# First-batch value sums by block: values as the stationary operand, masks as the streaming one

## The chip, the cores and the metric

The kernel runs on one core of a Trainium2 chip. The time is the device time of one execution in microseconds (us). The engines are named as in the profile: PE is TensorE's matmul, PEld its weight load, DVE is VectorE, ACT is ScalarE, POOL is GpSimd, SP is SyncE, which here issues the DMAs. They run side by side; each takes its own instructions strictly in the order in which they were written, and waits where an operand is not there yet.

## The reference

Attention over 4 batches x 8 heads x 768 positions x 64 dimensions, each query seeing the keys within 16 positions and one summary for each block of 32 keys, followed by a feed-forward network on 3072 tokens. `moe(...)` is x @ w_in, then h * tanh(softplus(h)), then @ w_out.

```
k_sum = k.reshape(B, H, nb, block, D).max(axis=3)       # 24 blocks of 32
v_sum = v.reshape(B, H, nb, block, D).mean(axis=3)
scores = concat([where(|i-j| < 16, q k^T / 8, -1e9), q k_sum^T / 8 + log(32)])
a = softmax(scores)
out = moe(concat([v, v_sum]) weighted by a)
```

The change bears on `v_sum` of the first batch alone.

## The kernel before

Work is cut into units: a chunk `c` of 256 positions and a pair of heads `hp` (4 pairs, so 128 value columns). The first two chunks (group 0, 512 tokens) are prepared by functions of their own before the feed-forward steps can start. From some 46 us on, PE works through feed-forward steps (`ph`: `ff_in`, L445; `po`: `ff_out`, L473) with the attention of the later groups between them. The weights come as 64-bit words that DVE and ACT turn into a high and a low part; the low part is the last step (`G`, `lower_weight`, L176). The steps for one piece of weights are `f` (`scale_weight`, ACT, L151), `B` and `C` (DVE, L155 and L159), `cl` (`clamp_weight`, DVE, L163, which needs `f`), `E` (DVE, L168), `hi` (`upper_weight`, ACT, L173, which needs `E`), `G`.

The order is written out by hand as a list of words, `order`; each word is one call, and each engine gets its instructions in that order. The words that matter here:

- `vm0` to `vm3`: `first_value_sums` (L262). For head pair 0 to 3 it sums the values by block with matmuls on PE: 8 windows of 64 positions (96 rows with their margins) and 2 pieces of 128 positions.
- `vc0` to `vc3`: `first_value_summary` (L272). ACT copies the 24 sums x 128 columns out of PSUM into the last 24 rows of a tile `vm` whose other 96 rows POOL has set to zero at the start (`zeroed`, L204).
- `X0` to `X3`: `att_values` (L402 to L418). It needs that tile as the stationary operand of its L411 matmuls, and the transposed weights `pt`.
- `T`: `att_transpose` (L390), 4 transposes on PE out of POOL's normalised rows (`nm`, L384); `pc`: the copy of its result on ACT (L394); `a` and `b` before the pair's number are the two chunks.
- `S`: scores (L336, L338), `ttr`: their maxima on DVE (L353), `exp`: exponentials on ACT (L364), `rs`: divisors on DVE (L379, L380), `xh`, `xl`: high and low part of X (ACT L427, DVE L428).

In the list the stretch reads `vm0 lv2 hi0 rsa2 ttr9 G0 km3 vm1 vc0 Ta1 nm8 B1 X0 T8 rsb1 S3 nma2 expb2 exp9 lvw8 vc1 lv3 C1 f1 nmb1 cl1 ...`.

Of the kernel before, what the change touches and what calls it, by code (L numbers as in the profile page):

```python
# [58 lines left out]
def fused_kernel(ctx: ExitStack, tc: tile.TileContext, q0, qk, kt, v0, vw, vs, w_in, w_out, out):  # L59
    nc = tc.nc  # L60
    PS = bass.MemoryType.PSUM

# [119 lines left out]

    blocks = first_att.tile([P, NW + NR, NB], F32, tag="blocks", name="blocks", bufs=1)
    nc.gpsimd.memset(blocks, 1.0 / BLK)
    for part, step, at0 in ((blocks[:, :NW], QT, -WIN), (blocks[:, NW:], P, TG)):
# [1 line left out]
        nc.gpsimd.affine_select(
            out=part, in_=part, pattern=[[step, n], [-BLK, NB]], base=at0, channel_multiplier=1,  # L190
            compare_op=ALU.is_ge, fill=0.0)
# [3 lines left out]
    part = blocks[:, :NW]
    nc.gpsimd.affine_select(
        out=part, in_=part, pattern=[[0, NW], [0, NB]], base=-WIN, channel_multiplier=1,
        compare_op=ALU.is_ge, fill=0.0)
    nc.gpsimd.affine_select(
        out=part, in_=part, pattern=[[0, NW], [0, NB]], base=WIN + QT - 1, channel_multiplier=-1,  # L200
        compare_op=ALU.is_ge, fill=0.0)


    zeroed = []  # L204
    for hp in range(HP):
        zeroed.append(att.tile([KA, P], F32, tag="vm", name=f"vm0_{hp}", bufs=HP))
        nc.gpsimd.memset(zeroed[hp][0:KW], 0.0)
# [356 lines left out]
    order = """  # L564
        lk0 lk1 km1 km0 lqk8 lq0 S0 lq1 ttra0 S1 lk2 ttrb0 expa0 ttra1 lqk9 kc9 kc8 expb0 lw0 km2 rsa0 ttrb1 rsb0 S8
        nma0 Ta0 lq2 nmb0 ttr8 lv0 expa1 expb1 S2 f0 B0 rsa1 C0 pca0 lv1 cl0 Tb0 lk3 lw1 ttra2 ttrb2 E0 exp8 rs8 lq3
        expa2 nma1 pcb0 vm0 lv2 hi0 rsa2 ttr9 G0 km3 vm1 vc0 Ta1 nm8 B1 X0 T8 rsb1 S3 nma2 expb2 exp9 lvw8 vc1 lv3 C1 f1
        nmb1 cl1 pca1 Tb1 rsb2 pc8 ttra3 E1 rs9 xh0 pcb1 vm2 ttrb3 lw2 X1 expa3 X8 hi1 xl0 G1 vc2 lqk11 nmb2 Ta2 nm9 Tb2
        xh1 T9 xl1 expb3 lqk10 vm3 rsa3 nma3 pca2 pcb2 X2 xh8 ls12 lvw9 kc11 lw3 f2 Ta3 rsb3 B2 nmb3 C2 vc3 xh2 Tb3 kc10
        pca3 xl8 cl2 E2 pcb3 hi2 S10 xl2 km12 ttr10 X3 pc9 xh3 X9 exp10 G2 xl3 ls13 ttr11 B3 lw4 ph0 f3 ph1 C3 exp11 ph2  # L570
        cl3 xh9 mi0 E3 km13 xl9 hi3 ah0 rs10 ph3 mi1 lw5 ah1 B4 G3 al0 f4 C4 cl4 E4 mi2 al1 hi4 nm10 B5 G4 po0 mi3 f5 C5
        lvw11 po1 T10 ph4 cl5 E5 lqk13 lqk12 lt12 hi5 vq12 ph5 ah3 ah2 al3 rs11 pc10 kc12 lw6 kc13 G5 f6 B6 nm11 ls15
        lvw10 al2 C6 lw7 S12 mi4 cl6 E6 km15 X10 mi5 ttr12 ah4 hi6 xh10 lw8 G6 f7 T11 ttr13 po2 B7 po3 cl7 C7 exp12 E7
        pc11 exp13 lt15 vq15 ph6 al4 hi7 B8 rs12 ah5 ph7 mi6 G7 dv12 al5 lqk14 nm12 po4 lw9 f8 ls14 ah6 po5 C8 xl10 X11
        cl8 al6 E8 km14 hi8 lw10 mi7 lqk15 T12 rs13 G8 ah7 xh11 B9 lvw12 C9 f9 po6 cl9 nm13 lt13 E9 lw11 hi9 pc12 B10
        al7 G9 kc15 f10 ph8 C10 mi8 xl11 ph9 cl10 po7 kc14 mi9 ah8 E10 S14 hi10 lw12 ah9 al8 ttr14 T13 ttr15 po8 G10
        exp14 ph10 al9 vq13 f11 exp15 B11 dv13 mi10 C11 cl11 rs15 ph11 E11 ah10 po9 al10 hi11 B12 lqk16 G11 rs14 X12
        mi11 ah11 lqk17 f12 pc13 C12 lt14 xh12 al11 nm15 cl12 lvw13 E12 po10 X13 hi12 xl12 kc16 T15 xh13 lw13 po11 vq14
        lw14 dv14 G12 pc15 B13 ph12 f13 ph13 cl13 C13 xl13 mi12 E13 dv15 nm14 kc17 ah12 B14 T14 hi13 lvw15 mi13 S16 al12
        lvw14 G13 ah13 lqk18 f14 lw15 al13 po12 X15 ttr16 C14 exp16 cl14 E14 rs16 ttr17 kc18 hi14 po13 pc14 X14 G14 ph14  # L580
        B15 C15 exp17 nm16 xh14 xh15 xl15 rs17 nm17 f15 mi14 lvw17 xl14 cl15 E15 ph15 hi15 T17 ah14 lvw16 ph16 mi15 ah15
        G15 al15 T16 ph17 pc17 al14 lqk19 kc19 X17 pc16 mi16 po14 po15 xh17 ah16 mi17 ah17 ph18 al16 oc0 oc1 mi18 X16
        xl17 xh16 ah18 al18 xl16 lvw19 al17 lvw18 po16
    """.split()
# [119 lines left out]
```

## Time and profile before

| | us |
|---|---|
| median of 3 runs (636.45, 639.64, 639.69) | 639.64 |
| the profiled execution | 638.28 |
| its span from the first to the last instruction | 636.6 |
| PE busy | 618.0 |
| DVE busy | 289.1 |
| ACT busy | 270.8 |
| POOL busy | 74.7 |
| granted clock of PE, mean over the span | 0.997 |

An average over the span hides two different stages. Up to some 123 us DVE is busy nearly all the time, and ACT for much of it; behind that PE alone is. A busy PE is not PE at its peak, since a matmul's record reaches from its start to the modelled end of its pipeline; the pace of matmuls is read from the distance of their starts.

### The profile page before, as it was taken

To read this page: it belongs to the slowest core of one execution; us is meant where nothing else is said; L and a number is where in the kernel's file an instruction comes from. 1 tells how busy PE (TensorE), PEld (TensorE's weight loads), DVE (VectorE), ACT (ScalarE), POOL (GpSimd) and SP (SyncE) were. 2 spreads that over 40 slices of the span, in tenths; PEclk is the share of its full clock that TensorE was granted. 3 is DMA by queue.
4 is the path that set the end of the run, shared out by engine and by line. 5 is a ranking of instruction groups with operands and counts; after the bars stand their busy time and mean duration, and the time that the engine had idled before them with its cause. 6 is when DMAs were issued, how large, how long until landed. Compare 5 with 4: busy or idle time off the path is not lost.

```text
span 636.6 us, 10992 instructions
## 1 busy us (share of the span) xinstructions
PE 618.0 (97%) x4272; PEld 509.4 (80%) x4272; DVE 289.1 (45%) x817; ACT 270.8 (43%) x659; POOL 74.7 (12%) x119
## 2 busy tenths in 40 slices
...
GB/s 269 243 271 280 217 214 196 236 178 82 79 7 115 57 139 115 219 1 96 58 40 95 93 132 141 96 96 96 66 96 71 26 32 1 66 1 0 1 0 67
DMA packets 31780, 68.24 MB, mean 107 GB/s; under 512 B 6768, under 2 KB 11632, under 8 KB 31728
## 3 DMA queue, kind: packets, MB, share of 16 engines
...
q8 instruction: 34, 0.56, 0.4%
q14 instruction: 18, 0.15, 0.1%
HBM read 59.11 MB, written 6.29 MB: 103 GB/s over the span
## 4 chain that ended last, share of the span: by engine, by line
PE 80%; DVE 6%; ACT 1%; issue 1%; DVEq 0%
PE po L473 37%; PE ph L445 36%; PE x_ps L417 3%; PE sc L332 2%; PE pt_ps L390 2%; DVE w L159 1%; DVE al L463 1%; DVE w L155 1%; DVE w_f L163 1%; DVE w_f L168 1%; DVE w_early_out_lo L176 1%; ACT pr L364 0%; DVE vq L280 0%; DVE km L259 0%; DVE pr L353 0%
## 5 line engine op out<-in xcount | busy, mean ns | idle before, releaser
L452 ACT ACTIVATE a<-ph 128x512 f32<-128x512 f32 x96 | 57.2, 597 | 245.0 <-PE ph L445 163.1
L461 DVE CAST ah<-a 128x512 fp32r<-128x512 f32 x80 | 34.5, 431 | 232.5 <-ACT a L452 231.1
L384 POOL TENSOR_TENSOR pr<-pr,rs 128x480 f32<-128x480 f32 x48 | 54.9, 1144 | 354.9 <-DVE rs L380 292.0
L473 PE MATMUL po<-w_early_out_hi,ah 128*128 128x512 f32 x240 | 94.8, 395 | 0.0
L445 PE MATMUL ph<-xh,w_early_in_hi 128*128 128x512 f32 x240 | 94.1, 392 | 0.0
L473 PE MATMUL po<-w_early_out_hi,al 128*128 128x512 f32 x240 | 93.3, 389 | 0.5 <-DVE al L463 0.4
L473 PE MATMUL po<-w_early_out_lo,ah 128*128 128x512 f32 x240 | 93.2, 388 | 0.0
L445 PE MATMUL ph<-xh,w_early_in_lo 128*128 128x512 f32 x240 | 93.1, 388 | 0.0
L445 PE MATMUL ph<-xl,w_early_in_hi 128*128 128x512 f32 x240 | 93.1, 388 | 0.0
L364 ACT ACTIVATE pr<-pr,nm 128x120 f32<-128x120 f32 x192 | 73.2, 383 | 10.0 <-DVE nm L353 9.8
L463 DVE TENSOR_TENSOR al<-a,ah 128x512 fp32r<-128x512 f32 x96 | 68.0, 710 | 4.0 <-ACT ah L461 1.3
L473 PE MATMUL po<-w_late_out_hi,ah 128*128 128x512 f32 x144 | 56.8, 395 | 0.0
L445 PE MATMUL ph<-xh,w_late_in_hi 128*128 128x512 f32 x144 | 56.7, 393 | 0.0
L445 PE MATMUL ph<-xh,w_late_in_lo 128*128 128x512 f32 x144 | 56.0, 389 | 0.5 <-DVE w_late_in_lo L176 0.5
L473 PE MATMUL po<-w_late_out_lo,ah 128*128 128x512 f32 x144 | 56.0, 389 | 0.0
L473 PE MATMUL po<-w_late_out_hi,al 128*128 128x512 f32 x144 | 55.9, 388 | 0.0
L445 PE MATMUL ph<-xl,w_late_in_hi 128*128 128x512 f32 x144 | 55.8, 388 | 0.0
L473 PEld LDWEIGHTS po<-w_early_out_hi,ah 128*128 128x128 f32 x240 | 45.0, 188 | 10.7 <-issue 1.9
L473 PEld LDWEIGHTS po<-w_early_out_hi,al 128*128 128x128 f32 x240 | 45.1, 188 | 10.0 <-DVE al L463 1.2
L445 PEld LDWEIGHTS ph<-xh,w_early_in_lo 128*128 128x128 f32 x240 | 45.1, 188 | 9.4
L473 PEld LDWEIGHTS po<-w_early_out_lo,ah 128*128 128x128 f32 x240 | 45.1, 188 | 9.3
L445 PEld LDWEIGHTS ph<-xh,w_early_in_hi 128*128 128x128 f32 x240 | 45.1, 188 | 8.9
...
## 6 DMA issues: line engine op xcount, KB each, us to landing
...
```

The costliest lines, as they stand in the source:

```text
L155: nc.vector.tensor_scalar(out=x, in0=x, scalar1=29, scalar2=None, op0=ALU.logical_shift_right)
L159: nc.vector.scalar_tensor_tensor(out=x, in0=high, scalar=SIGN, in1=x, op0=ALU.bitwise_and, op1=ALU.bitwise_or)
L332: nc.tensor.matmul(ps[h][row, at0:at0 + KA], u["qk"][r, s, h * QT:(h + 1) * QT], u["qk"][r, s, P:], start=True, stop=True)
L364: nc.scalar.activation(pr[:, s, :], pr[:, s, :], AF.Exp, scale=-1.0, bias=nm[:, s:s + 1], accum_out=sm[:, s:s + 1])
L384: nc.gpsimd.tensor_mul(u["p"], u["p"], u["r"].unsqueeze(2).broadcast_to([P, NQ, KA]))
L390: nc.tensor.transpose(ps[:KA, s * P:(s + 1) * P], u["p"][:, s, :], ident)
L417: nc.tensor.matmul(x, u["v"][0:rows, s, d], pt, start=(c >= CG), stop=(c >= CG or s == NQ - 1))
L445: nc.tensor.matmul(turned(ph), w[:, cc * P:(cc + 1) * P], turned(x[:, cc, :]), start=(cc == 0 and n == 0), stop=(cc == NCC - 1 and n == 2))
L452: nc.scalar.activation(a, st[g, fc], AF.Mish)
L461: (nc.scalar.copy if g == 0 else nc.vector.tensor_copy)(ah, a)
L463: return lambda: nc.vector.tensor_sub(al, a, ah.bitcast(F32))
L473: nc.tensor.matmul(turned(po[g][t]), a[:, tok], turned(w), start=(fc == 0 and n == 0), stop=(fc == NFC - 1 and n == 2))
```

## The change

A summing matmul had the masks (`blocks`, 24 columns) as stationary operand and the values (128 columns) as the streaming one, and all 10 of a head pair accumulated in one PSUM tile of 24 x 128. Now the values are stationary, in 4 groups of 32 columns, and the mask streams, 2 columns for a window and 4 for a piece of 128 positions: 40 matmuls for a head pair, each complete by itself, into a tile of 128 x 24. That result lies the other way round, so three steps follow where one copy was: `vd` (`first_sums_copy`, ACT) copies it behind 96 columns of zeros in an SBUF tile `sums`, `vt` (`first_sums_turn`, PE) transposes that to 120 x 128, and `vc` (ACT) copies all 120 rows to SBUF, zeros with them. POOL's preparation shrinks: masks of 128 x 8 in place of 128 x 240 with two selects fewer, and two zeroed tiles in place of four.

```diff
+    blocks = first_att.tile([P, 2, each], F32, tag="blocks", name="blocks", bufs=1)
...
+    turned_sums = [first_att.tile([P, KA], F32, tag=f"sums{k}", name=f"sums{k}", bufs=1) for k in range(2)]
+    for t in turned_sums:
+        nc.gpsimd.memset(t[:, 0:KW], 0.0)
...
         ps = sums_ps[hp] = att_psum(0, f"vm_ps0_{hp}")
+        at = 0
         for j in range(NW + NR):
-            nc.tensor.matmul(ps[KW:KA, 0:P],
-                             *((blocks[0:KW, j, :], units[j // NQ, hp]["v"][:, j % NQ, :]) if j < NW else
-                               (blocks[:, j, :], t[:, j - NW, :])),
-                             start=(j == 0), stop=(j == NW + NR - 1))
+            if j < NW:
+                v, m = units[j // NQ, hp]["v"][:, j % NQ, :], blocks[0:KW, 0, 0:QT // BLK]
+            else:
+                v, m = t[:, j - NW, :], blocks[:, 1, :]
+            n = m.shape[1]
+            for d in range(0, P, COLS):
+                nc.tensor.matmul(ps[d:d + COLS, at:at + n], v[:, d:d + COLS], m, start=True, stop=True)
+            at += n
+
+    def first_sums_copy(hp):
+
+        nc.scalar.copy(turned_sums[hp % 2][:, KW:KA], sums_ps.pop(hp)[:, 0:NB])
+
+    def first_sums_turn(hp):
+
+        ps = sums_ps[hp] = att_psum(0, f"vt_ps0_{hp}")
+        nc.tensor.transpose(ps[:KA, 0:P], turned_sums[hp % 2], ident)

     def first_value_summary(hp):

-        vm = zeroed[hp][KW:KA]
-        summary[0, hp].append(vm)
-        nc.scalar.copy(vm, sums_ps.pop(hp)[KW:KA, 0:P])
+        zeroed[hp] = att.tile([KA, P], F32, tag="vm", name=f"vm0_{hp}", bufs=HP)
+        nc.scalar.copy(zeroed[hp], sums_ps.pop(hp)[:KA, 0:P])
+        summary[0, hp].append(zeroed[hp][KW:KA])
...
-        expa2 nma1 pcb0 vm0 lv2 hi0 rsa2 ttr9 G0 km3 vm1 vc0 Ta1 nm8 B1 X0 T8 rsb1 S3 nma2 expb2 exp9 lvw8 vc1 lv3 C1 f1
+        expa2 nma1 pcb0 vm0 vd0 lv2 hi0 rsa2 ttr9 G0 vt0 km3 vm1 vd1 vc0 Ta1 nm8 B1 X0 T8 rsb1 S3 nma2 expb2 vt1 exp9
```

In the order list `vd` and `vt` are put in for each head pair, and nothing else moves. On the engines this looks as follows at the places that matter. First ACT, before, around the copies of head pairs 0 and 1 (L394 is `pc`, L173 `hi0`, L276 `vc0` and `vc1`, L364 the exponentials, L151 `f1`):

```order
10 L394 COPY pt_0_381<-pt_ps_0_388 120x512
11 L173 CAST w_early_in_hi<-w_f 128x1024
12 L276 COPY vm_0_141<-vm_ps_0_431 24x128
13 L364 ACTIVATE pr_2_405,sm_2_544<-pr_2_405,nm_2_406 128x120 x4
14 L364 ACTIVATE pr_1_450,sm_1_549<-pr_1_450,nm_1_451 128x120 x4
15 L276 COPY vm_1_143<-vm_ps_1_459 24x128
16 L151 ACTIVATE w_f<-w_0_396 128x1024
17 L394 COPY pt_1_567<-pt_ps_1_471 120x512
```

And the same place of ACT now (line numbers are those of the changed file: L273 is `vd`, L283 `vc`, L152 `f1`):

```order
10 L402 COPY pt_0_375<-pt_ps_0_382 120x512
11 L273 COPY sums_139<-vm_ps_0_425 128x24
12 L174 CAST w_early_in_hi<-w_f 128x1024
13 L273 COPY sums_140<-vm_ps_1_486 128x24
14 L283 COPY vm_0_528<-vt_ps_0_482 120x128
15 L372 ACTIVATE pr_2_399,sm_2_603<-pr_2_399,nm_2_400 128x120 x4
16 L372 ACTIVATE pr_1_475,sm_1_610<-pr_1_475,nm_1_476 128x120 x4
17 L283 COPY vm_1_618<-vt_ps_1_608 120x128
18 L152 ACTIVATE w_f<-w_0_390 128x1024
19 L402 COPY pt_1_629<-pt_ps_1_530 120x512
20 L402 COPY pt_0_639<-pt_ps_0_560 120x512
```

Two short copies have come in, one ahead of `hi0` and one behind it, and `vc1`, which `f1` stands behind, now reads `vt_ps_1` in place of `vm_ps_1`. Where `vt_ps_1` is made is seen on PE. PE before, from the sums of head pair 0 to X0 and T8:

```order
115 L267 MATMUL vm_ps_0_431<-vw_0_326,blocks 24x128 x8
116 L267 MATMUL vm_ps_0_431<-v_0_328,blocks 24x128 x2
117 L267 MATMUL vm_ps_1_459<-vw_1_383,blocks 24x128 x8
118 L267 MATMUL vm_ps_1_459<-v_1_385,blocks 24x128 x2
119 L390 MATMUL pt_ps_1_471<-ident,pr_1_259 120x128 x4
120 L411 MATMUL x_ps_0_480<-pt_0_381,vm_0_141 64x256 x2
121 L417 MATMUL x_ps_0_480<-pt_0_381,vw_0_326 64x64 x8
122 L411 MATMUL x_ps_0_480<-pt_0_381,vm_0_141 64x256 x2
123 L417 MATMUL x_ps_0_480<-pt_0_381,vw_0_326 64x64 x8
124 L390 MATMUL pt_ps_0_501<-ident,pr_0_320 120x128 x4
```

PE now, the same place (L278 is `vt`, L268 the sums, L398 `T`, L419 and L425 X):

```order
115 L268 MATMUL vm_ps_0_425<-blocks,vw_0_320 32x2 x32
116 L268 MATMUL vm_ps_0_425<-blocks,v_0_322 32x4 x8
117 L278 MATMUL vt_ps_0_482<-ident,sums_139 120x128
118 L268 MATMUL vm_ps_1_486<-blocks,vw_1_377 32x2 x32
119 L268 MATMUL vm_ps_1_486<-blocks,v_1_379 32x4 x8
120 L398 MATMUL pt_ps_1_530<-ident,pr_1_253 120x128 x4
121 L419 MATMUL x_ps_0_539<-pt_0_375,vm_0_528 64x256 x2
122 L425 MATMUL x_ps_0_539<-pt_0_375,vw_0_320 64x64 x8
123 L419 MATMUL x_ps_0_539<-pt_0_375,vm_0_528 64x256 x2
124 L425 MATMUL x_ps_0_539<-pt_0_375,vw_0_320 64x64 x8
125 L398 MATMUL pt_ps_0_560<-ident,pr_0_314 120x128 x4
```

The transposition of head pair 0 stands between the two passes of sums, so the second pass waits for ACT's copy of the first. That of head pair 1 has gone behind X0, T8 and the scores of pair 3 (their last two rows stand first here), where `vt_ps_1` is row 158:

```order
156 L344 MATMUL sc_3_1_569<-ks_3_387,q_3_414 64x96
157 L346 MATMUL sc_3_1_569<-km_3_484,q_3_414 64x24
158 L278 MATMUL vt_ps_1_608<-ident,sums_140 120x128
159 L398 MATMUL pt_ps_1_631<-ident,pr_1_276 120x128 x4
160 L268 MATMUL vm_ps_2_653<-blocks,vw_2_467 32x2 x32
161 L268 MATMUL vm_ps_2_653<-blocks,v_2_469 32x4 x8
```

Before, the sums of pair 1 that `vc1` copies were complete ahead of Ta1 and X0; now their transposition is some 30 rows further down on PE.

## Rows read from the trace of the kernel before

**Rows 1.** The page: busy time of PE, share of the span, instructions.
```profile
PE 618.0 (97%) x4272; PEld 509.4 (80%) x4272; DVE 289.1 (45%) x817; ACT 270.8 (43%) x659; POOL 74.7 (12%) x119
```

**Rows 2.** Windows: stretch, length, busy PE, PEld, DVE, ACT, POOL; granted clock, DMA share, GB/s.
```profile
20.70:46.00 25.30, 25.30 (x402) 21.34 (x401) 24.00 (x81) 21.29 (x64) 10.44 (x9) 0.96 0.84 258
46.00:64.00 18.00, 17.91 (x80) 14.57 (x81) 17.75 (x30) 13.41 (x30) 2.91 (x3) 1.00 0.84 281
64.00:122.70 58.70, 56.02 (x359) 44.99 (x358) 57.31 (x103) 40.81 (x78) 11.58 (x9) 1.00 0.66 217
```

**Rows 3.** Chain that ended last, 60 to 135 us: start, length, what.
```profile
121.47 1.23 DVE w_late_in_lo L176
122.73 5.27 PE ph L445 x22
```

**Rows 4.** Timeline of PE: start, us, engine, line, operation, tiles, shape, count.
```profile
20.75 2.76 PE L267 MATMUL vm_ps<-vw,blocks 96*24 96x128 f32 x16
...
23.78 1.91 PE L267 MATMUL vm_ps<-vw,blocks 96*24 96x128 f32 x16
...
26.06 0.65 PE L390 MATMUL pt_ps<-ident,pr 128*120 128x128 f32 x4
26.64 0.65 PE L411 MATMUL x_ps<-pt,vm 120*64 120x256 f32 x4
...
28.59 0.65 PE L390 MATMUL pt_ps<-ident,pr 128*120 128x128 f32 x4
29.18 0.42 PE L336 MATMUL sc<-ks,q 64*64 64x96 f32 x8
...
30.49 0.65 PE L390 MATMUL pt_ps<-ident,pr 128*120 128x128 f32 x4
```

**Rows 5.** The same timeline of PE: two runs of small matmuls, each with its successor.
```profile
27.13 0.64 PE L417 MATMUL x_ps<-pt,vw 96*64 96x64 f32 x16
27.59 0.60 PE L411 MATMUL x_ps<-pt,vm 120*64 120x256 f32 x4
...
29.39 0.28 PE L338 MATMUL sc<-km,q 64*64 64x24 f32 x8
29.48 0.41 PE L336 MATMUL sc<-ks,q 64*64 64x96 f32 x8
```

**Rows 6.** Timeline of ACT, 22 to 36 us; in brackets idle time ahead and releaser.
```profile
22.59 0.56 ACT L394 COPY pt<-pt_ps 120x512 f32<-120x512 f32 x1
23.62 1.05 ACT L173 CAST w_early_in_hi<-w_f 128x1024 fp32r<-128x1024 f32 x1 [0.46 <-DVE w_f L168]
24.69 0.26 ACT L276 COPY vm<-vm_ps 24x128 f32<-24x128 f32 x1
24.97 0.40 ACT L364 ACTIVATE pr<-pr,nm 128x120 f32<-128x120 f32 x1
...
28.14 0.26 ACT L276 COPY vm<-vm_ps 24x128 f32<-24x128 f32 x1
28.42 1.20 ACT L151 ACTIVATE w_f<-w 128x1024 f32<-128x1024 f32 x1
...
35.44 0.59 ACT L427 CAST xh<-x_ps 128x512 fp32r<-128x512 f32 x1 [0.66 <-PE x_ps L417]
```

**Rows 7.** Timeline of DVE, 28 to 38 us.
```profile
28.30 1.20 DVE L159 SCALAR_TENSOR_TENSOR w<-w 128x1024 uint32<-128x1024 uint32 x1
29.64 1.24 DVE L163 TENSOR_SCALAR w_f<-w_f 128x1024 f32<-128x1024 f32 x1
...
37.57 0.79 DVE L379 TENSOR_SCALAR rs<-sm 128x4 f32<-128x4 f32 x1 [0.40 <-ACT pr L364]
```

**Rows 8.** Timeline of POOL, 24 to 32 us.
```profile
28.46 1.88 POOL L384 TENSOR_TENSOR pr<-pr,rs 128x480 f32<-128x480 f32 x1 [1.52 <-DVE rs L380]
```

**Rows 9.** Windows of PE alone: stretch, length, busy time, granted clock, DMA share, GB/s.
```profile
15.50:19.00 3.50, 1.82 (x54) 1.00 1.07 221
19.00:22.40 3.40, 3.40 (x40) 0.51 1.05 334
```

More of the change, by code (lines that the diff above doesn't have):

```diff
@@ L23 @@
 QT = 64
+COLS = 32
 KW = QT + 2 * WIN
@@ L181, in fused_kernel @@
     first_more = begin.enter_context(tc.tile_pool(name="first_more", bufs=HP, side="right"))
-    blocks = first_att.tile([P, NW + NR, NB], F32, tag="blocks", name="blocks", bufs=1)
+    each = P // BLK
+    blocks = first_att.tile([P, 2, each], F32, tag="blocks", name="blocks", bufs=1)
     nc.gpsimd.memset(blocks, 1.0 / BLK)
-    for part, step, at0 in ((blocks[:, :NW], QT, -WIN), (blocks[:, NW:], P, TG)):
-        n = part.shape[1]
+    for k, at0 in enumerate((-WIN, 0)):
         nc.gpsimd.affine_select(
-            out=part, in_=part, pattern=[[step, n], [-BLK, NB]], base=at0, channel_multiplier=1,
+            out=blocks[:, k], in_=blocks[:, k], pattern=[[-BLK, each]], base=at0, channel_multiplier=1,
             compare_op=ALU.is_ge, fill=0.0)
         nc.gpsimd.affine_select(
-            out=part, in_=part, pattern=[[-step, n], [BLK, NB]], base=BLK - 1 - at0, channel_multiplier=-1,
+            out=blocks[:, k], in_=blocks[:, k], pattern=[[BLK, each]], base=BLK - 1 - at0, channel_multiplier=-1,
             compare_op=ALU.is_ge, fill=0.0)
[L195 to L207, printed above, removed]
+    turned_sums = [first_att.tile([P, KA], F32, tag=f"sums{k}", name=f"sums{k}", bufs=1) for k in range(2)]
+    for t in turned_sums:
+        nc.gpsimd.memset(t[:, 0:KW], 0.0)
+    zeroed = {}
     summary = {}
@@ L553, in fused_kernel @@
         "vm": number(first_value_sums), "vc": number(first_value_summary),
+        "vd": number(first_sums_copy), "vt": number(first_sums_turn),
         "lw": number(load_weight), "f": number(scale_weight), "B": number(low_bits), "C": number(sign_bits),
@@ L571, in fused_kernel @@
[L571 to L580, printed above, removed]
@@ L581, in fused_kernel @@
-        B15 C15 exp17 nm16 xh14 xh15 xl15 rs17 nm17 f15 mi14 lvw17 xl14 cl15 E15 ph15 hi15 T17 ah14 lvw16 ph16 mi15 ah15
-        G15 al15 T16 ph17 pc17 al14 lqk19 kc19 X17 pc16 mi16 po14 po15 xh17 ah16 mi17 ah17 ph18 al16 oc0 oc1 mi18 X16
-        xl17 xh16 ah18 al18 xl16 lvw19 al17 lvw18 po16
+        expa2 nma1 pcb0 vm0 vd0 lv2 hi0 rsa2 ttr9 G0 vt0 km3 vm1 vd1 vc0 Ta1 nm8 B1 X0 T8 rsb1 S3 nma2 expb2 vt1 exp9
+        lvw8 vc1 lv3 C1 f1 nmb1 cl1 pca1 Tb1 rsb2 pc8 ttra3 E1 rs9 xh0 pcb1 vm2 vd2 ttrb3 lw2 X1 expa3 X8 hi1 vt2 xl0 G1
@@ new lines, in fused_kernel @@
+        vc2 lqk11 nmb2 Ta2 nm9 Tb2 xh1 T9 xl1 expb3 lqk10 vm3 vd3 rsa3 nma3 pca2 pcb2 X2 xh8 ls12 lvw9 kc11 lw3 f2 Ta3
+        rsb3 B2 vt3 nmb3 C2 vc3 xh2 Tb3 kc10 pca3 xl8 cl2 E2 pcb3 hi2 S10 xl2 km12 ttr10 X3 pc9 xh3 X9 exp10 G2 xl3 ls13
+        ttr11 B3 lw4 ph0 f3 ph1 C3 exp11 ph2 cl3 xh9 mi0 E3 km13 xl9 hi3 ah0 rs10 ph3 mi1 lw5 ah1 B4 G3 al0 f4 C4 cl4 E4
+        mi2 al1 hi4 nm10 B5 G4 po0 mi3 f5 C5 lvw11 po1 T10 ph4 cl5 E5 lqk13 lqk12 lt12 hi5 vq12 ph5 ah3 ah2 al3 rs11
+        pc10 kc12 lw6 kc13 G5 f6 B6 nm11 ls15 lvw10 al2 C6 lw7 S12 mi4 cl6 E6 km15 X10 mi5 ttr12 ah4 hi6 xh10 lw8 G6 f7
@@ new lines, in fused_kernel @@
+        T11 ttr13 po2 B7 po3 cl7 C7 exp12 E7 pc11 exp13 lt15 vq15 ph6 al4 hi7 B8 rs12 ah5 ph7 mi6 G7 dv12 al5 lqk14 nm12
+        po4 lw9 f8 ls14 ah6 po5 C8 xl10 X11 cl8 al6 E8 km14 hi8 lw10 mi7 lqk15 T12 rs13 G8 ah7 xh11 B9 lvw12 C9 f9 po6
+        cl9 nm13 lt13 E9 lw11 hi9 pc12 B10 al7 G9 kc15 f10 ph8 C10 mi8 xl11 ph9 cl10 po7 kc14 mi9 ah8 E10 S14 hi10 lw12
+        ah9 al8 ttr14 T13 ttr15 po8 G10 exp14 ph10 al9 vq13 f11 exp15 B11 dv13 mi10 C11 cl11 rs15 ph11 E11 ah10 po9 al10
+        hi11 B12 lqk16 G11 rs14 X12 mi11 ah11 lqk17 f12 pc13 C12 lt14 xh12 al11 nm15 cl12 lvw13 E12 po10 X13 hi12 xl12
```

10 lines of the change are left out of this document (6 added, 4 removed).

## The prediction

> **What bounds the kernel now.** I read the page first. PE is busy 97% of the span [rows 1], so at first sight every us taken from PE should show in the time. The windows by stage say otherwise. From 20.7 to 46 us, where all four passes of value sums lie, DVE is busy 24.0 of 25.3 us, from 46 to 64 us 17.75 of 18.0, and from 64 to 122.7 us 57.3 of 58.7, while PE stands idle for 0.1 and 2.7 us in the last two [rows 2]. The chain of waits tells which of the two sets the end: up to 122.7 us it runs mostly over DVE's weight steps, the last of them the low part of a late weight (121.47 to 122.70), which a `ph` matmul on PE waits for; from there on it is PE alone [rows 3]. So the end is the moment at which DVE has worked through its list up to there, plus PE work that this change doesn't touch. PE time saved before 46 us reaches the end only if it makes DVE earlier, and whatever makes DVE later is paid in full, but for the small gaps that DVE still has.
>
> Then the timelines. On PE a pass of sums lasts from one start to the next: 20.75 to 23.78 for pair 0 (3.0 us) and 23.78 to 26.06 for pair 1 (2.3 us) [rows 4]. Pair 0 is longer since the granted clock was 0.51, that is the level of 1.2 GHz, from 19.0 to 22.4 us, after a stretch in which PE was busy 1.8 of 3.5 us [rows 9]. On ACT and DVE the reader is to see how tightly both are coupled: `vc1` ends at 28.4, `f1` starts at 28.42 and lasts 1.20, and `cl1` on DVE starts at 29.64, just when `f1` ends, while DVE's own step ahead of it, `C1`, was done at 29.5 [rows 6, 7]. So any delay of `f1` over 0.1 us is a delay of DVE.
>
> **The change part by part.** *The sums themselves.* A matmul leaves two records, as the 8 windows of a pass left 16 [rows 4], so the 40 of a pass now leave 80. No row shows a stream of 2 or 4 columns. The nearest are the summary scores, 24 columns in 4 tiles side by side: 8 records in 0.09 us, 11 ns each; farther off, 64 columns in two groups: 16 records in 0.46 us, 29 ns [rows 5]. This bounds a pass between 0.9 and 2.3 us. I take 15 ns, so 1.2 us: near the first, since the new ones too have four groups side by side and few columns, with a little added because all 96 or 128 rows are loaded each time. At 1.2 GHz it is double.
>
> The Trainium skill (TensorEngine Tiling (Array Packing), Instruction Overhead) states that every matmul carries about 60 cycles of overhead, so that one streaming column takes as long as 60, and advises against gaining from a dimension that is already small. An estimate by that page: 60 cycles at 2.4 GHz are 25 ns, 2.0 us for a pass, and the end would be some 2.5 us later in place of the 1.1 below. The trace disagrees as far as it goes: the 24-column records start 11 ns apart [rows 5].
>
> *PE's account.* Four passes took 3.0 + 3 x 2.3 = 9.9 us; they now take 2.05 (the first partly at the low clock, below) + 3 x 1.2 = 5.7, and four transpositions come in. Four of the same kind last 0.58 us from their start to the next step's [rows 4], so 0.15 each, 0.6 in all. PE saves some 3.6 us, in a place where it then waits for others.
>
> *The new steps on ACT.* A copy of 128 columns takes 0.26 us and one of 512 takes 0.56 [rows 6]; by the line through them 24 columns take 0.18. For `vd` I take the upper end, 0.26, four times; `vc` has the same 128 columns as before on more partitions and stays at 0.26. Alone this is 1.0 us of ACT.
>
> *The order, followed through.* The first pass starts at 20.75 as before; by 22.4 at 30 ns it has done 55 records, the other 25 at 15 ns end it at 22.8. ACT is in `pcb0` until 23.15 [rows 6], so `vd0` runs from 23.15 to 23.4, inside the 0.46 us in which ACT now waits for DVE, and `hi0` still starts at 23.62. `vt0` ends at about 23.75 (0.3 with the tail of a single one). The second pass follows from 23.55 and is readable at 24.95. ACT is free of `hi0` at 24.67; `vd1` lasts until 25.2, `vc0` until 25.45, and the exponentials start at 25.48 in place of 24.97. X0, which needs `vc0`, starts at 25.5 in place of 26.64. X0 and `T8` take 1.95 + 0.59 us and the scores of pair 3 up to 1.31 [rows 4], which makes 29.35 before PE comes to `vt1`, and 29.65 for its result. ACT has ended its exponentials (3.17 us long [rows 6]) at 28.65 and stands at `vc1`, 1.0 us idle. Queued behind it are `f1`, `pcb` and `xh` copies and all later exponentials. `vc1` ends at 29.95, `f1` at 31.15, and `cl1` starts 1.5 us later than its 29.64. This is the one new wait that I expect to cost something: before, `vc1` read a sum that PE had finished ahead of X0; now its input lies behind X0, `T8` and `S3`.
>
> *What is given back.* ACT was idle 0.66 us ahead of `xh1` [rows 6], and DVE 0.40 ahead of a divisor at 37.57 that waits for exponentials [rows 7]. DVE's 1.5 falls to 1.1 there; ACT's 1.5 becomes 1.5 - 0.66 + 0.26 (`vd2`) = 1.1 as well, so that the divisor doesn't wait longer. For pairs 2 and 3 the shorter passes hide their own new steps: PE can't be early there, since the next transposition waits for POOL until 28.46 + 1.88 = 30.34 [rows 8], and `vd2` stands behind a `pc` copy that is itself late by then. From 46 to 122.7 DVE is idle for only 1.6 us [rows 2] in small gaps, of which I count nothing.
>
> *Costed at nothing.* POOL's shorter preparation: the other masks it prepares are read by DVE only after the first scores, and those wait for a load. The added PSUM tiles: their places were last used by steps done long before. The loads that wait for a pass to end come about 1 us earlier. If the cover on POOL or PSUM were gone, tenths of a us would be at stake.
>
> **Sum.** 638.28 (profiled execution; 636.6 of it the span) + 1.1 = 639.4. The profiled execution lies 1.36 below the median of 639.64, within the runs' own spread from 636.45 to 639.69; on the scale of the median the forecast is 640.7. A change under 0.5%, 3.2 us, can hardly be told from none here.
>
> **The rivals.** *A, a floor under small matmuls:* each record costs the 29 ns of the 64-column rows. Then the first pass is readable at 24.1, `hi0` starts 0.7 late, the second pass ends at 27.0, X0 starts at 27.55, `vt1` is done at 31.7, `cl1` starts at 33.2, 3.55 late, less 0.4: 638.28 + 3.1 = 641.4, on the median's scale 642.8. For it speaks that each record has a weight load of its own; against it the 11 ns [rows 5]. The Trainium skill's rule on overhead, named above, describes this mechanism; its own estimate lies a little under it.
>
> *B, the four groups don't overlap, slower:* the 29 ns of two groups side by side are 58 ns for one [rows 5]. A pass is 4.6 us, the first ends at about 26.2, the second at 31.3, and `vt1` at 36; `cl1` comes 7.9 us late, less 0.4: 645.8, or 647.1. From 29 ns a record on, the loss passes 3.2 us. Against it: the score rows do run side by side in four tiles.
>
> *C, the low clock comes again:* PE now has waits at 22.8 to 23.5 and from 29.7 to 30.5, and another ahead of X1. The clock fell before after a stretch that was half idle [rows 9]; 3.4 us at half speed cost 1.7. If they fall on X0 to `S3` or on X1, they add to the wait of ACT: 1.1 + 1.7, so 641.1, or 642.4.
>
> *D, PE's saving reaches the end, faster:* 638.28 - 3.6 = 634.7, or 636.0. It would need DVE to follow PE in the first 46 us; DVE's 95% there [rows 2] and the order of its steps speak against it.
>
> **How the numbers follow.** Forecast 0.50, C 0.17, A 0.13, B 0.10, D 0.10. The likeliest is 640.7. A range from 636.5 to 644.0 takes in A, C and the bounds of the record's price up to 29 ns, and leaves out B and D, 2 in 10. Slower by over 0.5%: B, and a good half of A and part of C, 0.20. Faster: most of D, 0.07. Within: 0.73.
>
> **What would show it.** Right: passes of 1.0 to 1.5 us on PE at full clock; ACT idle about 1 us ahead of the second copy from a `vt` tile, with PE as the releaser; `clamp_weight` near 31 us in place of 29.64; the `ph` matmul of 122.73 about 1 us later, and everything behind it as before. Wrong: starts of records 25 ns or more apart; a granted clock of half after 22.4 us; DVE's clamp at 29.6 or earlier; or the `ph` matmul earlier than 122.7, which would mean that DVE's list was not what bound.

## The result, and the profile after

| | before | changed |
|---|---|---|
| median of 11 runs each (lowest to highest), us | 639.05 (636.45 to 640.15) | 644.92 (642.05 to 646.53) |
| ratio, with its 95% interval | 1 | 1.0100 (1.0081 to 1.0119) |
| profiled execution, its span, us | 638.28, 636.6 | 646.50, 644.8 |
| granted clock, mean over the span | 0.997 | 0.983 |

The changed kernel is 1% slower, 5.9 us by the medians. That is outside the range given (636.5 to 644.0), on the slow side. The profiled execution is one of its slower ones, 1.6 us above the median.

Two lines of the page after, the one that answers to [rows 1] and the one of a DMA queue (packets, MB, share of 16 engines):

```profile
PE 619.3 (96%) x4516; PEld 509.6 (79%) x4516; DVE 288.2 (45%) x817; ACT 270.3 (42%) x663; POOL 72.4 (11%) x115
...
q8 instruction: 36, 0.59, 0.4%
```

Busy times hardly differ from before. What grew is the count of PE's records, by 244 (4272 before), and a queue that carries instructions: 36 packets of 0.59 MB, where the page of before has 34 and 0.56. Now the windows by stage, with the columns of [rows 2]; the last one ends 8.3 us later than there, since the stage does.

```profile
20.70:46.00 25.30, 18.71 (x524) 15.09 (x525) 18.12 (x67) 15.90 (x60) 9.88 (x8) 0.76 0.90 260
46.00:64.00 18.00, 18.00 (x180) 15.01 (x176) 15.98 (x35) 14.72 (x34) 2.08 (x3) 0.91 0.49 166
64.00:131.00 67.00, 63.72 (x394) 50.77 (x392) 64.42 (x111) 44.28 (x84) 13.48 (x11) 1.00 0.69 225
```

In the first of these windows PE's busy time fell from 25.3 to 18.7 us, and DVE's from 24.0 to 18.1, ACT's from 21.3 to 15.9. All three engines stand still more, and the granted clock is 0.76 where it was 0.96. That is no saving: the window is as long as before while the stage now reaches to 53.4 us, and the missing work has moved behind 46 us. From 20.7 us to the first `ph` matmul PE is busy 26.1 us, where it was 25.2, and DVE 23.6, where it was 23.9. From 64 us on DVE is busy 64.4 of 67.0 us, nearly as before, so what is late by then stays late. The chain that ended last shows how much of it is left at its end (start, length, what; it answers to [rows 3]):

```profile
129.69 1.23 DVE w_late_in_lo L177
130.96 5.27 PE ph L453 x22
```

The `ph` matmul of 122.73 starts at 130.96, 8.2 us later, and the span is 8.2 us longer: from there on all is as before. Most of it is lost ahead of the first `ph` matmul of all, which starts at 53.37 in place of 45.90, 7.5 us later. PE's timeline tells where (columns as in [rows 4]; rows of the scores left out):

```profile
21.69 1.03 PE L268 MATMUL vm_ps<-blocks,vw 96*32 96x2 f32 x64
22.57 0.37 PE L268 MATMUL vm_ps<-blocks,v 128*32 128x4 f32 x16
23.39 0.47 PE L278 MATMUL vt_ps<-ident,sums 128*120 128x128 f32 x1 [0.45 <-ACT sums L273]
23.79 0.70 PE L268 MATMUL vm_ps<-blocks,vw 96*32 96x2 f32 x34
26.38 0.55 PE L268 MATMUL vm_ps<-blocks,vw 96*32 96x2 f32 x27 [1.89 <-issue]
...
27.12 1.11 PE L398 MATMUL pt_ps<-ident,pr 128*120 128x128 f32 x4
28.16 1.12 PE L419 MATMUL x_ps<-pt,vm 120*64 120x256 f32 x4
...
31.78 1.03 PE L398 MATMUL pt_ps<-ident,pr 128*120 128x128 f32 x4
...
34.05 0.32 PE L278 MATMUL vt_ps<-ident,sums 128*120 128x128 f32 x1
...
34.74 0.70 PE L268 MATMUL vm_ps<-blocks,vw 96*32 96x2 f32 x63
35.27 0.19 PE L268 MATMUL vm_ps<-blocks,v 128*32 128x4 f32 x2
...
37.69 0.51 PE L425 MATMUL x_ps<-pt,vw 96*64 96x64 f32 x10 [0.58 <-issue]
...
44.19 0.29 PE L268 MATMUL vm_ps<-blocks,v 128*32 128x4 f32 x12 [1.61 <-issue]
```

Three things are to be seen. The records are cheap: in the pass of pair 2, at full clock, 63 start within 0.53 us, 8.4 ns each. PE stops in the middle of a pass, 1.89 us in the second and 1.61 in the last, and "issue" says that it waited for nothing that another engine owed it. And X0 to `vt1`, with no new step in it, takes 28.16 to 34.05, 5.9 us, where it took 26.64 to 30.49 [rows 4]. The window of the middle of that stretch (length, busy PE, granted clock, DMA share, GB/s):

```profile
27.10:32.60 5.50, 5.50 (x54) 0.50 0.50 103
```

PE is busy all the time and runs at 1.2 GHz. By the trace's clock records the half level lasts from 15.5 to 32.6 us, and from 46.2 to 49.7; before, only from 19.1 to 22.5 in this stretch. The first fall, at 15.5, lies ahead of the first changed matmul at 21.69; what differs from before is that the clock then stays low for 17 us and not for 3.4. ACT, and the clamp on DVE, which answers to the rows of `vc1`, `f1` and `cl1` in [rows 6, 7]:

```profile
27.25 0.18 ACT L273 COPY sums<-vm_ps 128x24 f32<-128x24 f32 x1 [2.23 <-PE vm_ps L268]
...
34.41 0.27 ACT L283 COPY vm<-vt_ps 120x128 f32<-120x128 f32 x1 [3.79 <-PE vt_ps L278]
34.57 1.14 ACT L152 ACTIVATE w_f<-w 128x1024 f32<-128x1024 f32 x1
```

```profile
35.74 0.69 DVE L164 TENSOR_SCALAR w_f<-w_f 128x1024 f32<-128x1024 f32 x1 [5.60 <-ACT w_f L152]
```

The wait that was forecast is there, in its place and with its releaser: ACT stands at `vc1` for `vt1`, `f1` behind it, and DVE's clamp behind `f1`. It is 6.1 us late where 1.5 was forecast.

### The profile page after: what moved, and what is told of

It reads as the page before. It is cut to its first block, busy times and chain, and to the rows that moved or that the text cites. A ratio compares the mean times of both kernels' runs of the same rounds, so it can differ in the third digit from the quotient of the medians.

```text
span 644.8 us, 11483 instructions
## 1 busy us (share of the span) xinstructions
PE 619.3 (96%) x4516; PEld 509.6 (79%) x4516; DVE 288.2 (45%) x817; ACT 270.3 (42%) x663; POOL 72.4 (11%) x115
## 4 chain that ended last, share of the span: by engine, by line
PE 81%; DVE 10%; DMA 3%; ACT 2%; issue 2%; SPq 0%; DVEq 0%; ACTq 0%
PE po L481 36%; PE ph L453 35%; PE x_ps L425 3%; PE pt_ps L398 3%; PE sc L340 2%; DVE w L160 1%; DMA w<-w_in 1%; DVE w L156 1%; DVE w_f L169 1%; DMA vsum<-vs 1%; DVE al L471 1%; DVE w_f L164 1%; DMA q<-qk 1%; DVE w_early_out_lo L177 1%; ACT pr L372 1%
## 5 line engine op out<-in xcount | busy, mean ns | idle before, releaser
L469 DVE CAST ah<-a 128x512 fp32r<-128x512 f32 x80 | 34.6, 433 | 232.1 <-ACT a L460 230.8
```

Of the source, the lines that this page charges most:

```text
L469: (nc.scalar.copy if g == 0 else nc.vector.tensor_copy)(ah, a)
```

## Experiments

Three theories came out of this, and each has a share in the trace. **W**, the wait by order: ACT's new copies stand ahead of steps that others need. **C**, the half clock: PE works X0, `T8` and `S3` at 1.2 GHz. **The fetch** (theory F in the expectations): the many short instructions run ahead of the instruction stream, which arrives in packets, and PE stops until the next one is there. Each kernel was timed beside the kernel before on the same chip. The table gives the difference of the medians, the ratio's interval, the granted clock as a mean over the spans of all its runs, and from the profiled execution the start of the first `ph` matmul and PE's stops by issue from 20 to 46 us. Where an edit moves words of the order list, its diff shows only the words around the move.

| kernel | us over before | ratio, 95% | clock | first `ph` | stops, us |
|---|---|---|---|---|---|
| before | 0 | | 0.996 | 45.90 | 0 |
| changed | +5.9 | 1.0081 to 1.0119 | 0.987 | 53.37 | 4.1 |
| e1 | +6.7 | 1.0084 to 1.0122 | 0.987 | 51.01 | 3.2 |
| e2 | +6.8 | 1.0086 to 1.0120 | 0.987 | 51.66 | 0 |
| e3 | +7.4 | 1.0101 to 1.0140 | 0.984 | 52.31 | 3.8 |
| e4 | +5.4 | 1.0068 to 1.0107 | 0.994 | 50.66 | 2.3 |
| e5 | +4.7 | 1.0051 to 1.0093 | 0.990 | 53.61 | 5.7 |
| e6 | +5.4 | 1.0073 to 1.0122 | 0.987 | 50.61 | 0 |
| e8 | +2.5 | 1.0033 to 1.0069 | 0.996 | 48.10 | 0 |
| e9 | +0.4 | 0.9995 to 1.0025 | 0.996 | 46.25 | 0 |
| e10 | +3.1 | 1.0046 to 1.0102 | 0.995 | 49.17 | 0 |
| e11 | +5.7 | 1.0077 to 1.0138 | 0.987 | 49.94 | 0 |
| e12 | +7.7 | 1.0098 to 1.0145 | 0.987 | 56.37 | 0 |
| e13 | +5.3 | 1.0068 to 1.0110 | 0.992 | 49.17 | 3.9 |
| e15 | +5.1 | 1.0055 to 1.0094 | 0.992 | 50.81 | 5.4 |
| e16 | +5.8 | 1.0059 to 1.0098 | 0.992 | 50.73 | 5.0 |
| e17 | +7.5 | 1.0090 to 1.0132 | 0.986 | 52.92 | 0 |
| e18 | +7.0 | 1.0075 to 1.0123 | 0.984 | 53.06 | 0 |

In all 18 profiled executions the whole time less the start of the first `ph` matmul lies between 591.9 and 593.1 us (638.28 - 45.90 = 592.4 before, 646.50 - 53.37 = 593.1 changed). So whatever any of these kernels loses in its profiled execution, it loses ahead of that matmul, to within some 1 us.

**e1, e3: the wait by order, one step at a time.** e1 moves `vc1` behind `f1`, e3 moves `vt1` ahead of `T8`.

```diff
-        lvw8 vc1 lv3 C1 f1 nmb1
+        lvw8 lv3 C1 f1 vc1 nmb1
```

```diff
-        X0 T8 rsb1 S3 nma2 expb2 vt1 exp9
+        X0 vt1 T8 rsb1 S3 nma2 expb2 exp9
```

> The changed kernel with one word moved: vc1 (ACT's copy of pair 1's turned sums) behind f1 instead of ahead of it. Theory W (the wait of ACT at vc1 for the transposition that lies behind X0, T8 and S3 on PE is what makes DVE late): the 5.6 us wait of DVE's clamp for f1 shrinks to 1 to 2 us and about 4 us of the 6 come back, 640 to 641.5. Rival P (PE itself is late, by the stop in the stream of small matmuls and the half clock, and everything that needs S3 or X1 is late with it): the wait moves to the maxima of pair 3 or to xh1, and the time stays at 643.5 to 645.

> The changed kernel with one word moved on PE: vt1 directly behind X0 instead of behind T8, S3. Theory W: vc1's input is there 2 to 4 us earlier, DVE's wait for f1 falls from 5.6 to 2 or 3 us, 641 to 643. Rival P: no gain over 1 us, since T8 and S3 still come at the same time.

Both did at their place what they should: the clamp starts at 28.54 and 30.07. Neither gained anything, as rival P had it. In e1 `vc1` now waits 3.07 us and DVE 1.74 for scores; in e3 PE stops for 3.16 us inside X1, ACT waits 5.07 for `vt2` behind it, and DVE 4.20 for ACT. Theory W alone is refuted: with that wait gone, the next late thing of PE takes its place.

**e2: one column group**, so 40 matmuls for four pairs in place of 160, with the same order.

```diff
-COLS = 32
+COLS = 128
```

> The changed kernel with COLS = 128: the values are loaded as one group of 128 columns, 10 matmuls a pass in place of 40, same result, same order list. Theory F (PE's stop of 1.9 and 1.6 us within a pass is the fetch of its instructions, which 160 short ones outrun): with 40 instructions a pass the stops inside vm_ps are gone, a pass takes about 2.2 us again (20 records at about 0.11), and PE, busier, keeps the full clock for longer; 641 to 642.5, the wait of f1 for vt1 staying at 1.5 to 3 us. Rival (the stop has nothing to do with how many instructions there are): a stop of over 1 us in the pass of pair 1 stays and the time is 644 or more.

The stops by issue are gone, as the fetch theory says, and the time is no better, which neither side expected: the clamp waits 6.99 us for `f1`, and the half clock lasts from 20.9 to 31.1 us. Not one cause alone, then.

**e4, e9: work added to the kernel before**, its results unused: 30 matmuls of 32 x 2 for each pass in e4, 3 of 24 x 128 in e9.

```diff
+        for j in range(30):
+            d = j % 3 * 32
+            nc.tensor.matmul(ps[d:d + 32, 256 + 2 * (j // 3):258 + 2 * (j // 3)],
+                             units[0, hp]["v"][:, 0, d:d + 32], blocks[0:KW, 0, 0:2], start=True, stop=True)
```

```diff
+        for j in range(3):
+            nc.tensor.matmul(ps[0:24, 128 + 128 * j:256 + 128 * j], blocks[0:KW, j, :],
+                             units[0, hp]["v"][:, 0, :], start=True, stop=True)
```

> The kernel before with 30 added matmuls of 32 x 2 ahead of each pass of sums (their result is not used), so that a pass has the 80 records of the changed kernel, but no vd, no vt and the old order. Theory F: a stop of 1 to 2 us by issue appears in two or three of the passes, the passes get 0.6 us longer by the matmuls themselves, vc0 and X0 come about 2 us later, and the time rises by 1 to 3 us. Rival (small matmuls cost only their own time): no stop, passes 0.6 us longer, time within 1 us of the kernel before.

> The kernel before with 3 added matmuls of 24 x 128 ahead of each pass (result not used), some 0.65 us of PE each pass as the 30 tiny ones took, but 12 PE instructions in place of 120. If PE's time up to 46 us is slack, as the prediction had it: within 1 us of the kernel before. If it counts in full: 2 to 3 us more. Theory F: at least 2 us under the kernel with the tiny ones, which was 5.4 us slower than before.

This pair is the clearest. Three wide matmuls lengthen a pass by 0.65 us and cost nothing that can be measured (+0.4, interval -0.05% to +0.25%): PE's time as such is slack here. Thirty tiny ones take no more of PE (some 0.5 us at 8.4 ns a record) and cost 5.4 us, more than was expected. PE's timeline of e4 has what they bring:

```profile
24.68 0.34 PE L268 MATMUL vm_ps<-blocks,vw 96*32 96x2 f32 x16 [1.49 <-issue]
...
43.31 0.62 PE L271 MATMUL vm_ps<-vw,blocks 96*24 96x128 f32 x4 [0.85 <-issue]
```

The second stop hits a wide matmul of the kernel before itself, so it is not the tiny ones' own cost. Counted from the start of the trace in PE's and PEld's records, the stops stand at record 706 and 1474 here, at 706, 1218 and 1474 in the changed kernel, always a multiple of 256 apart, whatever instruction lies there. In all eight kernels that have stops from 20 to 46 us these stand at 706, 962, 1218 or 1474, or one record earlier. At each one a packet of 16,384 bytes is under way on the instruction queue: in the changed kernel they start at 23.78, 35.17 and 41.74, last 1.0 to 1.2 us, and PE goes on 1.3 to 1.6 us after their end. 36 packets for 2 x 4516 records are 251 records each, which fits one packet for each stretch of 256. The two kernels differ in how fast PE gets through such a stretch. Before, the one from record 450 to 706 lasts from 19.1 to 29.7 us; the packet starts 3.8 us after its begin and has ended at 24.0. In the changed kernel PE goes through it from 20.2 to 24.5 us; the packet starts 3.6 us after its begin, much as before, and ends at 24.8, too late. The two stops are 2.3 of the 4.8 us by which the first `ph` of e4 is late. In that execution the half level also lay from 26.6 to 30.0 us, over Ta1 and half of X0, so the 5.4 us are the whole effect of the added matmuls and not that of the stops alone. In e9's profiled execution the clock was full from 14.9 us on, but over all its runs it is that of before, 0.996.

**e5, e6: four words moved against the waits of order**, with four groups and with one: `vc1` behind `f1`, `vt1` behind X0, `vd3` behind `f2`, `vc3` behind `xh2`.

```diff
-        X0 T8 rsb1 S3 nma2 expb2 vt1 exp9 lvw8 vc1 lv3 C1 f1
+        X0 vt1 T8 rsb1 S3 nma2 expb2 exp9 lvw8 lv3 C1 f1 vc1
...
-        vm3 vd3 rsa3 nma3 pca2 pcb2 X2 xh8 ls12 lvw9 kc11 lw3 f2 Ta3 rsb3 B2 vt3 nmb3 C2 vc3 xh2
+        vm3 rsa3 nma3 pca2 pcb2 X2 xh8 ls12 lvw9 kc11 lw3 f2 vd3 Ta3 rsb3 B2 vt3 nmb3 C2 xh2 vc3
```

> The changed kernel with five words moved so that no copy stands in ACT's queue ahead of work whose input is there: vc1 behind f1, vt1 directly behind X0, vd3 behind f2, vc3 behind xh2. Theory W (waits in queue order, which the two single moves only shifted from pairs 0 and 1 to pairs 2 and 3): both stretches are mended and the time falls to 639.5 to 641.5. Theory F (stops in the stream of short instructions on PE, and the low clock): the stops stay, 643 to 645.

> The same order with the values as one group of 128 columns, 40 PE instructions a pass in place of 160. Theory F: without the stops only the longer chain of copies is left, 639 to 641, and below the kernel with four groups by 2 us or more. Theory W alone: the same as with four groups within 1 us.

e5 keeps the stops (5.7 us) and the half clock (18.3 to 32.0) and is 4.7 us over before, 643.0, where the fetch theory had it. e6 went against that theory: it has no stops, and at 643.7 it is no faster than e5. Its second pass of sums falls to the half clock and ACT waits 2.88 us for it.

**e8: the wait by order alone, in the kernel before**: `vm1` moved behind `S3`, so that `vc1` waits as the prediction had it.

```diff
-        km3 vm1 vc0 Ta1 nm8 B1 X0 T8 rsb1 S3 nma2
+        km3 vc0 Ta1 nm8 B1 X0 T8 rsb1 S3 vm1 nma2
```

> The kernel before with one word moved: vm1 behind S3, so that vc1 on ACT waits for a sum that lies behind X0, T8 and S3 on PE, and nothing else is changed. Theory W: f1 and DVE's clamp come 2 to 2.5 us later than 29.6 and the time rises by 1.5 to 2.5 us over the kernel before. Theory F: an order wait without small matmuls costs under 1 us.

```profile
31.73 0.26 ACT L276 COPY vm<-vm_ps 24x128 f32<-24x128 f32 x1 [4.65 <-PE vm_ps L267]
```

+2.5 us. The clamp starts at 33.18, 3.5 us later, and the first `ph` 2.2 later. This is the mechanism that the prediction named, and a clamp that is 3.5 us late costs 2.5, where the prediction's 0.4 given back would leave 3.1; the interval (2.1 to 4.4 us) holds both. In this execution the half level lay from 25.1 to 28.5 us, so a part of the 3.5 may be the clock's; over all runs the clock is that of before.

**e10: e6 with the clock held up** by 6 full matmuls of 128 x 120 ahead of each of the first two passes, their result unused.

```diff
+        for j in range(6 if hp < 2 else 0):
+            nc.tensor.matmul(ps[:, 128:128 + KA], ident, base, start=True, stop=True)
```

> The kernel with all placed words and one group, plus 6 full matmuls (128 x 120, results not used, some 1.3 us of PE) ahead of the passes of pairs 0 and 1. Theory C (the granted clock fell to half from 24.4 to 31.2 us in that kernel because PE's passes stream only 2 or 4 columns, and the half speed of X0 and T8 costs DVE): the clock stays at full there, the time falls by 1 to 2.5 us to 641 to 642.5 though PE has 2.6 us more to do. Rival (the waits of ACT's copies alone set the time): the clock makes no difference and the added work costs, 643.5 to 646.

PE's timelines, first the second pass of e6, then that of e10:

```profile
23.85 2.93 PE L268 MATMUL vm_ps<-blocks,vw 96*128 96x2 f32 x16
26.64 0.99 PE L268 MATMUL vm_ps<-blocks,v 128*128 128x4 f32 x4
```

```profile
24.28 1.50 PE L261 MATMUL vm_ps<-base,ident 128*128 128x120 f32 x12
25.61 1.85 PE L270 MATMUL vm_ps<-blocks,vw 96*128 96x2 f32 x16
27.33 0.59 PE L270 MATMUL vm_ps<-blocks,v 128*128 128x4 f32 x4
27.77 0.63 PE L400 MATMUL pt_ps<-ident,pr 128*120 128x128 f32 x4
```

With more work on PE, and the clock at 1.00 from 20.7 to 46 us, the median is 2.6 us lower, the best of all kernels with swapped operands. By the ratios (1.0097 and 1.0074) it is 1.5, and the two intervals overlap, since two of e10's 7 runs lie at 645 to 647; its runs with a high clock are its short ones. The median lies at the fast end of theory C's range; what made the clock fall in e6, and why the added matmuls kept it up here, this run does not show.

**e11, e12, e13: the copies of sums moved further back** (`vd1` behind `expb2`, `vt1` behind `S3`, `vd2` behind `expa3`, and the moves of e5 for the rest), with one group, with one group and the full matmuls, and with four groups and these.

```diff
-        vm1 vd1 vc0 Ta1 nm8 B1 X0 T8 rsb1 S3 nma2 expb2 vt1 exp9 lvw8 vc1 lv3 C1 f1
+        vm1 vc0 Ta1 nm8 B1 X0 T8 rsb1 S3 nma2 expb2 vd1 exp9 lvw8 vt1 lv3 C1 f1 vc1
```

> The kernel with one group, with vd1 behind expb2 and vt1 behind S3, vd2 behind expa3, and the words of pair 3 and vc1 moved as before: now no new copy stands on ACT ahead of exponentials or hi. Theory W: the 2.9 and 1.5 us that ACT waited at the copies of pairs 1 and 2 are gone; 640 to 642. Theory C alone: the clock still falls to half for two stretches, 643 to 644.5.

> Both: the late copies and the full matmuls ahead of the passes of pairs 0 and 1. If the order waits and the clock are all that the kernel with few instructions lost, it is back at 638 to 640.5, within 0.4% of the kernel before; if it stays above 642, a cause is missing.

> The same with four groups of 32 columns, 160 PE instructions a pass. Theory F: with waits and clock mended only the stops of the instruction stream are left, 1.5 to 4 us above the kernel with one group. Rival: equal to it within 1 us, or below, since its passes are 1.5 us shorter.

None of them came near the kernel before. In e11 the wait moves on: ACT waits 4.17 us at `vc1` and DVE 2.99 for scores, and the half clock lasts from 21.2 to 31.5 us. e12 kept the half clock from 25.1 to 35.3 us in spite of the added matmuls, so it says nothing on the price of the clock; at 645.7 it is far over the 642 from which on a cause was to be missing. e13 was to be 1.5 to 4 us above it by the fetch theory and is 2.4 below, but the two differ in clock as well (0.992 and 0.987). In e13 the clock is full but for 34.6 to 38.1 us, the clamp starts at 28.02, early, and the stops are what is left:

```profile
34.48 0.30 PE L270 MATMUL vm_ps<-blocks,v 128*32 128x4 f32 x13 [2.96 <-issue]
```

It stands at record 1218 again; the changed kernel had there a matmul of X1, since e13 has other work ahead. With clock and clamp nearly in order 3.6 us are left in this execution (641.92 against 638.28) and 5.3 by the medians. PE's stops make 3.9 us there, so they are the likeliest reason, but no run takes them away from this kernel and keeps the rest.

**e15, e16: the clock held up in the changed kernel itself, and in e5**, by the edit of e10.

> The changed kernel in its own order, with 6 full matmuls of 128 x 120 (result unused, 0.3 to 0.6 us) ahead of the first two passes of sums and nothing else. Theory C (the half clock is a cause of its own, worth the 2.5 us that it was between e6 and e10): the granted clock from 20.7 to 46 us is near full and the time is 642.0 to 643.0. Rival, the theory that the half clock only fills what the stops of PE and the order make PE wait anyway: the clock is full, but the stops by issue and the wait ahead of vc1 stay and the time is 644.3 to 646. Third outcome: the clock falls all the same, as in e12; then the run says nothing on its price.

> e5 (the changed kernel with the five moved words, four column groups) with the same 6 full matmuls ahead of the first two passes. Against e5's 643.0: theory C gives 640.5 to 641.5, with stops by issue of 2 to 4 us left as the rest over the kernel before. The rival that the stops alone set the time gives 642.5 to 644.5 with a full clock.

Windows of e15 from 20.7 to 46 us, and its stops on PE:

```profile
20.70:46.00 25.30, 18.09 (x557) 15.22 (x557) 17.90 (x61) 16.73 (x59) 10.41 (x9) 0.93 0.83 254
```

```profile
24.61 0.59 PE L270 MATMUL vm_ps<-blocks,vw 96*32 96x2 f32 x52 [0.28 <-issue]
...
30.34 0.33 PE L346 MATMUL sc<-ks,q 64*64 64x96 f32 x4 [1.46 <-issue]
...
35.66 0.38 PE L270 MATMUL vm_ps<-blocks,v 128*32 128x4 f32 x13 [2.66 <-issue]
...
42.93 0.33 PE L270 MATMUL vm_ps<-blocks,vw 96*32 96x2 f32 x19 [0.96 <-issue]
```

The clock went from 0.76 to 0.93, and 0.8 us (1.7 by the ratios, 1.0100 and 1.0074) came back, just above the range of theory C; the stops stayed, 5.4 us of them. The intervals of the two kernels (1.0081 to 1.0119, 1.0055 to 1.0094) overlap. e16 gained nothing on e5 and lies in the rival's range, but its clock was not full: the half level lay from 33.6 to 40.5 us, and over all runs the clock rose only from 0.990 to 0.992. So it hardly tests the price of the clock.

**e17, e18: e6 with `vm1` right behind `vm0`**, with 6 and 3 full matmuls ahead of the first two passes, and bare.

```diff
-        pcb0 vm0 vd0 lv2 hi0 rsa2 ttr9 G0 vt0 km3 vm1 vd1
+        pcb0 vm0 vm1 vd0 lv2 hi0 rsa2 ttr9 G0 vt0 km3 vd1
```

> e10 with the second pass of sums right behind the first one, ahead of the transposition that waits for ACT, and 3 full matmuls in place of 6 ahead of the second pass. No stops by issue and, if the clock holds, only the order is left: theory W (what is left in e10, 3.1 us over the kernel before, is ACT's wait of 2.9 us at the second copy of sums for the second pass) gives a second pass that ends near 26.5 us, a wait of 1 to 1.6 us there, a clamp near 31 us and a time of 639.3 to 640.3, 1.3 to 2.3 over the kernel before. Rival, the longer work of ACT (four more copies) and the later passes set the rest: 640.7 to 641.5, as in e10.

> e17 without the full matmuls: what they do in this order. Theory C gives half clock again for some 7 us or more between 20.7 and 46 us, and 1.5 to 2.5 us more than e17, 641 to 642.5. Rival: the clock stays, since PE no longer waits between the two passes, and the time is e17's or 0.5 less.

e17 missed its range by 5 us, e18 by 2.4, and e18 shows why. A window of its PE, and its second pass of sums:

```profile
21.00:34.00 13.00, 13.00 (x85) 0.50 0.59 157
```

```profile
25.14 3.55 PE L268 MATMUL vm_ps<-blocks,vw 96*128 96x2 f32 x16
28.56 0.99 PE L268 MATMUL vm_ps<-blocks,v 128*128 128x4 f32 x4
29.41 0.45 PE L278 MATMUL vt_ps<-ident,sums 128*120 128x128 f32 x1
```

PE is busy for all of these 13 us, with no stop and no wait, and runs at 1.2 GHz: the pass takes 4.3 us (25.14 to 29.41) where e10's took 2.2 (25.61 to 27.77). ACT waits 3.15 us at `vd1` for it, the clamp 3.69 for `f1`. The clock had fallen at 17.0 us, after a stretch in which PE was busy 1.4 of 3.4 us, much as in [rows 9]; but then it did not rise for 17 us, in 13 of which PE had no wait at all. And in e17 it fell at 26.7 us straight after such a stretch without waits:

```profile
23.30:26.70 3.40, 3.40 (x32) 0.99 1.01 238
```

What I had taken for the reason of the half clock, PE's waits, is not needed for it. The rest of e10, +3.1, could not be put down to its order by this pair, because the clock fell in both.

**The clock over all runs.** Each run has its time and its mean clock. Taken as differences from the mean of its own kernel, over the 112 runs of the changed kernel and the experiments, 0.01 less of clock goes with 2.9 us more (correlation -0.66). The changed kernel's 0.987 against 0.996 would be 2.6 us of its 5.9. It is a share read from runs that differ by themselves, not a trial; a run with longer waits may also have a lower clock because of them.

## Why the prediction was wrong

- **What bounds the kernel: right.** Shorter passes brought nothing at the end (D falls), e9 shows that some added PE time costs nothing, and all that is lost ahead of the first `ph` matmul arrives at the end, to within some 1 us.
- **The price of the sums: too high.** 15 ns a record were taken, 8.4 measured at full clock; a pass of 1.2 us takes 0.68. At the half clock it was to be double; the first pass has 64 records in 0.88 us (21.69 to 22.57), 14 ns each. Rivals A (29 ns) and B (groups one after the other) fall. The Trainium skill (TensorEngine Tiling (Array Packing), Instruction Overhead) states about 60 cycles of overhead for every matmul, from which the prediction made an estimate of 25 ns a record. The runs show 8.4, or 17 for one of these matmuls, which leaves two records.
- **The new steps on ACT: right.** `vd` 0.18 us (0.26 was taken), `vc` 0.27 (0.26).
- **"The order, followed through": the step that failed.** Its places and releasers are as forecast, its times are not. `vt1` was to start at 29.35 and starts at 34.05, 4.7 us later. 2.7 of that stand ahead of X0 (28.16 in place of 25.5): the stop of 1.9 us in the second pass, and that pass and Ta1 at half clock (Ta1 takes 1.04 in place of 0.58). The other 2.0 are X0 to `S3` at half clock, 5.9 in place of 3.85. The step took PE to start each instruction as soon as its operands are there, and to run at full clock from 22.4 us on. So the clamp came 6.1 us late and not 1.5, and the time rose by 5.9 us and not by 1.1.
- **"What is given back": wrong in the changed kernel**, not contradicted by e8, where 3.5 us at the clamp became 2.5. Here nothing came back (6.1 us at the clamp, 7.5 at the first `ph`, 8.2 at the `ph` of 122.73), since the stops of pairs 2 and 3 follow: 1.61 us at 44.19, behind which ACT's `vd3` and `vc3` wait 2.28 and 2.41.
- **Rival C came true besides the forecast, and larger**: 1.7 us and the chance 0.17 were put on 3.4 us of half clock; the trace has 17. The fall after a stretch half idle, read from [rows 9], is not the only one: in e17 the clock fell after 3.4 us without a wait.
- **The stops by issue were in no rival.** Nothing in the profile of before shows one, but the counts were there: 160 matmuls, 640 records of PE and PEld, in place of 160.

**What is shown and what stays open.** Shown: many short instructions added to the kernel before cost 5.4 us (e4), as much PE time in few instructions nothing (e9), the wait by order alone 2.5 (e8), and PE's stops come with the record count. They don't add up, since ACT and DVE wait for whichever comes last, so mending one shows little (e1, e2, e3). Not shown: an exact split of the 5.9 us; what the half clock costs by itself, which only e10 and e15 could test, with intervals that overlap those of e6 and the changed kernel; what of e10's 3.1 is order; and why the added matmuls held the clock up in e10 and not in e12 or e17. Kernels without a single stop (e2, e6, e11) are as slow as the changed one, so the stops are not needed for a loss of this size. No run adds the new copies and transpositions alone to the kernel before. No kernel with the operands swapped came nearer to the time of the one before than 3.1 us.
